# Windowed attention and a SiLU feed-forward on one core: idle matmuls placed by hand, a first d_ff group over both visits' tokens, and Strassen's scheme one tile earlier

## The chip, the cores and the metric

The kernel runs on one core of a Trainium2 chip. A core has a matrix engine (TensorE, PE in the profile; its weight loads are shown as PEld), a vector engine (VectorE, DVE), an engine for activation functions (ScalarE, ACT), a general engine (GpSimd, POOL), and a queue engine (SyncE, SP). They run side by side, each through its own list of instructions in order, and wait for each other on semaphores. Data move between the main memory and the core by DMA. Matmul results land in PSUM, which the kernel sees as eight banks of 512 fp32 columns in 128 partitions. The metric is the time of one execution on the device in microseconds (us), as the median of several runs.

## The reference

```python
# q, k, v: [8 batches, 8 heads, 576 positions, 64]
scores = scale * np.matmul(q, k.transpose(0, 1, 3, 2))
rel = pos[:, None] - pos[None, :]
mask = (rel >= 0) & (rel < 64)                  # 64 positions back, causal
attn = softmax(np.where(mask, scores, -1e9))
x = np.matmul(attn, v) -> [4608 tokens, 512]    # heads side by side
h = x @ w_in                                    # 512 -> 2048
g = h * (1.0 / (1.0 + np.exp(-h)))              # SiLU
out = g @ w_out                                 # 2048 -> 512, float32
```

## The kernel before

**Attention in visits.** The 4608 tokens are 72 blocks of 64, nine to a batch. A visit takes three blocks (visits 0 to 3) or four (the others) through a chain: scores on TensorE (line 317, in 32-row tiles of the array), exponential on ScalarE (L324), mask on VectorE (L333; the first three visits have the mask added in PSUM by four bias matmuls, L309, instead), attention times values on TensorE (L350, in 32-column tiles), then on VectorE a reciprocal (L356), the normalisation (L361, which empties the PSUM banks) and a transpose called the crossing (L369), which writes the tokens into the buffer `bridge`. Q and K are loaded by GpSimd's DMA queue (the first rows by SP and ScalarE) and turned on VectorE (L296, L299). Odd and even blocks need V rows in two layouts, so half of the rows are copied (L279).

**Feed-forward in tiles.** A tile is 512 tokens (eight blocks); there are nine, 0 to 8. The first layer (L379) takes 16 groups of 128 d_ff columns, each the sum of four matmuls over d_model; SiLU follows on ScalarE (L386), into slots of the buffer `g`. Tile 0 is cut up, since its tokens arrive visit by visit: groups 0 to 3 take the 192 tokens of visit 0, then those of visit 1 (`add_halves`, 32 matmuls of 192 columns), other groups take tokens 0 to 383 at once, and the last 192 tokens come later. The second layer has two forms. The plain one (L389) is 64 matmuls of 512 columns a tile, with copies of the result from PSUM (L394). The fast one, Strassen's scheme over 2 x 2 blocks (tokens in two halves, d_ff in two halves, d_model in two halves), is seven products in place of eight, 112 matmuls of 256 columns (L421). It needs sums of weights (L405, once, VectorE), sums of activations (L412, 16 a tile, VectorE), copies of partial results (L424, VectorE or ScalarE) and joins (L431, L433, VectorE). Tiles 0 to 2 use the plain form, tiles 3 to 8 (`FAST`) the fast one.

**What sets the order.** `Plan` (lines 16 to 137) is a list scheduler in the kernel's own Python. Operations are put into classes, each a queue in order; at each moment every engine takes, from the heads of the classes it serves, the one with the lowest number `first` (by default the class's `rank`) whose dependencies are done, whose gate is open and whose PSUM banks are free. Each operation has an assumed duration, from which the plan gets its clock. The order that comes out is what is issued. Attention stages run among the matmuls of the feed-forward; scores may run up to two tiles ahead (`gate_scores`). Until the last visit is done attention owns banks 0 to 3 and the feed-forward has 4 to 7. The plan also counts TensorE's instructions in `code` (an operation's own number, 2 for a matmul and its weight load) and lets TensorE stall where `code` passes 193, 449, 705 and so on, unless the instructions from there on, asked for 256 earlier, have come.

**Idle matmuls.** Until the first layer begins TensorE is given matmuls on a tile of zeros whose results nobody reads (`warm`, L719, 512 columns; `burn`, L724, four narrow ones). In the kernel before they are fillers: a class of the lowest priority, taken whenever TensorE would have nothing else by the plan's clock. There are 23 calls of `burn`, ten of `warm`, and up to 90 more of `warm` until the first d_ff matmul is planned. As issued, 92 narrow and 20 wide ones stand ahead of visit 0's scores, 9 between its scores and its values, 6 between visit 1's, and 4 between visit 1's values and visit 2's scores.

Of the kernel before, what the change touches and what calls it, by code (L numbers as in the profile page):

```python
# [15 lines left out]
class Plan:  # L16
# [13 lines left out]
    def add(self, cls, us, fn, deps=(), lat=0.1, gate=None, code=2, dma=None, pool=None, table=None, first=None, slow=0.0):  # L30
        op = dict(us=us, first=self.rank[cls] if first is None else first, fn=fn, deps=[d for d in deps if d is not None],
                  lat=lat, gate=gate, dma=dma, pool=pool, table=table, code=code, seen=None, n=self.count, until=[], bank=None, cls=cls, slow=slow)
        self.count += 1
        self.queues.setdefault(cls, []).append(op)
        return op

    def add_filler(self, n, cls, us, fn, parts, *args, **kw):
        for _ in range(n):
            op = self.add(cls, us, None, *args, **kw)
            op["until"], op["fn"], op["parts"] = [op], lambda e, op=op: fn(op), parts  # L40
        self.count -= n
# [10 lines left out]
    def run(self):  # L52
# [10 lines left out]
        while left:  # L63
# [6 lines left out]
            while moved:  # L70
                moved = False
                for e in engines:
# [28 lines left out]
                    if e == "PE":  # L101
                        m = {"s": "rows", "v": "cols"}.get(c[0] if c in ("s", "v", "s0", "v0") else "", "full")
                        if m != mode:
                            mode, us = m, us + 0.1
                        for x in range(193, code + op["code"], 256):
                            if x >= code:
                                t = us * (x - code) / op["code"]
                                us += max(0.0, chunk.get(x, 0.0) - now - t)
                                chunk[x + 256] = max(now + t, chunk.get(x, 0.0)) + (5.6 if now < 25 else 2.5)
# [22 lines left out]
                    left -= not c.startswith("warm")  # L132
# [8 lines left out]
def kernel(ctx, tc, q, k, v, w_in, w_out, out):  # L141
# [12 lines left out]
    NBR = 32  # L154
    NK, NV, NES, NOB = 2, 3, 3, 2
    RING = list(range(33, 40, 2)) + list(range(1, 32, 2))
    FAST = range(3, NTT)
# [42 lines left out]
                  s=1, v=0, moe=99, warm=200, warm2=201, exp=1, mask=1, inverse=0, norm=0.1, cross=0.2, turn=-1.25, cast=-4,  # L200
                  prime=-9, s0=-5.5, v0=-5.6, exp0=-4.6, inverse0=-4.3, norm0=-4.24, cross0=-4.22, turn0=-4.23, copy=1.5, copy0=-4.05),
# [251 lines left out]
    def add_turns(b, c=None):  # L453
        for Q in range(2):
            for kk in range(2):
                op = p.add("turn0" if b == 0 else "turn", {"DVE": 0.27 if b == 0 else 0.24 + 0.06 * (PARTS[b][c][1] - PARTS[b][c][0]) if b == 1 else 0.78}, lambda _, kk=kk, Q=Q: turn(b, kk, Q, c),
                           ([rows_in[(b, kk, c, Q)]] if b < 2 else rows_in[(b, kk, Q)]) + s_last.get(b - NK, []) + [c_k[b % NK]],
                           first=0.25 if (b, c) == (1, 2) else None if b > 1 else None, gate=p.late([rows_in[(b, kk, c, Q)]] if b < 2 else rows_in[(b, kk, Q)], 0.7) if b else None)
# [13 lines left out]
    def add_copies(b):  # L472
        for g in range(4):
            for up in (True, False):
                v_sh[(b, g, up)] = p.add("copy" if b else "copy0", {"DVE": 0.3} if (b, g, up) == (0, 2, True) else {"DVE": 0.3} if b == 0 and g == 3 else {"ACT": 0.66} if b > 1 or (b == 0 and g) else {"ACT": 0.66, "DVE": 0.3},
                                         lambda e, up=up, g=g: copy_v(e, b, g, up), v_in[(b, g)][0:1] + v_last.get(b - NV, []),
# [59 lines left out]
    def add_visit(vi):  # L536
# [7 lines left out]
        s = p.add("s" + z, {"PE": 0.05 * ns + (0.85 if first else 0.1)}, None,  # L544
# [3 lines left out]
        vi["s"] = s  # L548
# [5 lines left out]
        if not first:  # L554
            ma = p.add("mask", {"DVE": 0.16 + 0.00053 * 256 * ns}, lambda _: masking(vi), [ex, c_mask])
        pv = p.add("v" + z, {"PE": 0.05 * ns + 0.1}, None, [ma] + need_v(vi), pool=("two0", "two1", "two0")[i] if i < 3 else "at",
                   gate=(lambda: moe[20][0]["seen"] is not None) if i == 2 else None)
        pv["fn"] = lambda _: values(pv, vi)
        pv["code"] = 16 * ns
# [5 lines left out]
                   [no] + [x for n in range(vi["n0"], vi["n0"] + vi["nb"]) for x in br_free.get(n - NBR, [])])  # L565
# [38 lines left out]
    def add_halves(fts, gt):  # L604
        first = {}
        for i in range(2):
            for ft in fts:
                for c in range(NDC):
                    op = p.add("moe", {"PE": 0.0036 + 192 / 2400}, None, [o_done[3 * i], win[(ft, c)]], pool=None if c or i else "mp0")
                    bank = first.setdefault(ft, op)  # L610
                    op["fn"] = lambda _, bank=bank, ft=ft, c=c, i=i: first_layer(bank, 0, ft, c, 192 * i, 192 * i + 192, 192 * i)
                    moe.append((op, 1, 1 if c == 0 and i == 0 else -1, 0))
                if i:
                    slot, si = gt[ft]
                    op = p.add("silu", {"ACT": 0.18 + 384 * 0.00083}, lambda _, bank=bank, slot=slot: silu(bank, slot, 0, 384), [op], table="silu")
                    si.append(op)
                    bank["until"] = [op]
# [99 lines left out]

    def warm(op):
        nc.tensor.matmul(ps[:, op["bank"][0], 0:128 * op["parts"]], lhsT=idle, rhs=idle.unsqueeze(1).to_broadcast([128, op["parts"], 128]),  # L719
                         start=True, stop=True)  # L720

    def burn(op):
        for j in range(4):
# [144 lines left out]
```

## Time and profile before

| | |
|---|---|
| median of 3 runs | 293.4 us (293.4 to 294.83) |
| the profiled execution | 291.75 us |
| its span, first to last instruction | 290.0 us |
| TensorE busy (share of the span) | 280.6 us (97%), 4019 matmuls |
| VectorE busy | 165.3 us (57%) |
| ScalarE busy | 167.9 us (58%) |
| GpSimd busy | 117.6 us (41%) |
| mean granted TensorE clock | 0.994 |

Times in the profile are us from the span's start unless marked ns. A row of a timeline or of a group names the engine, the operation, the tile written, an arrow, the tiles read, the shapes and a count; square brackets hold the idle time before it and what ended that. The chain is followed back from the last instruction: at each step to what released it, else to the instruction before it on its engine; its rows give start, length and what. "Issue" is time in which the engine waited for nothing that the profile shows. A row of stretches gives from:to and the length, then the engines' busy times. Some matmul records are missing from a trace, so counts can be a few short, and the length of a single matmul includes its way through the pipeline.

### The profile page before, as it was taken

The page shows a single profiled execution, that of the slowest core. Times are in us where ns is not written, and L with a number is a line of the kernel's source. Part 1 is how long each engine was busy: PE and PEld are TensorE (multiplying, and loading weights), DVE is VectorE, ACT ScalarE, POOL GpSimd, SP SyncE. Part 2 cuts the span into 40 slices and gives each one's busy share as a digit, 9 for nine tenths or more (in the row PEclk, how much of TensorE's full clock was granted, in tenths as well). Part 3 has the DMA queues.
Part 4 walks back from the last instruction along what each step waited for, and adds up shares of the span by engine and source line. Part 5 has one row for each costly group of instructions (what it writes and reads, how often), then busy time and mean ns, then how long its engine had stood idle before and what let it go on. Part 6 is the DMA issues. An engine that isn't in the chain of part 4 may idle for free.

```text
span 290.0 us, 9229 instructions
## 1 busy us (share of the span) xinstructions
PE 280.6 (97%) x4019; PEld 178.0 (61%) x4031; DVE 165.3 (57%) x306; ACT 167.9 (58%) x261; POOL 117.6 (41%) x181
## 2 busy tenths in 40 slices
PE   8789999999999999999999999999999999999995
PEld 4247764796544445447854785478547854784584
DVE  3583416992955258646874687459446944332433
ACT  2629871899747763768256844683468346416610
POOL 8965848989987988697500000000000000000000
PEclk9799999999999999999999999999999999999999
DMA  9999999999999999999961003000300030003013
GB/s 149 127 187 190 190 183 141 201 164 127 173 222 157 174 161 181 222 128 186 97 184 48 2 2 147 0 5 2 145 2 3 3 148 0 2 3 141 2 36 109
DMA packets 88840, 31.51 MB, mean 109 GB/s; under 512 B 75872, under 2 KB 84064, under 8 KB 88800
## 3 DMA queue, kind: packets, MB, share of 16 engines
q0 software_dynamic: 81600, 18.00, 67.3%
q1 hardware_dynamic: 6016, 11.75, 12.4%
q10 hardware_dynamic: 1184, 1.18, 1.4%
q8 instruction: 31, 0.51, 0.7%
q14 instruction: 9, 0.07, 0.1%
HBM read 36.70 MB, written 9.44 MB: 159 GB/s over the span
## 4 chain that ended last, share of the span: by engine, by line
PE 91%; DMA 3%; DVE 2%; ACT 1%; issue 1%; ACTq 0%; DVEq 0%
PE ps L379 42%; PE ps L421 26%; PE ps L389 12%; PE ps L350 4%; PE ps L317 4%; PE ps L719 2%; DMA gsum<-in_k_dram 2%; DMA natq<-in_q_dram 1%; DVE ob L361 1%; ACT e L324 1%; ACTq L263 0%; DVE qt L299 0%; ACT L386 0%; DVE kt L299 0%; DVE bridge L369 0%
## 5 line engine op out<-in xcount | busy, mean ns | idle before, releaser
L379 PE MATMUL ps<-bridge,w_in_sb 128*128 128x512 bf16 (+3 forms) x720 | 127.0, 337 | 0.4 <-ACT g L386 0.4
L386 ACT ACTIVATE g<-ps 128x512 bf16<-128x512 f32 (+3 forms) x176 | 89.7, 520 | 42.4 <-PE ps L379 41.2
L379 PEld LDWEIGHTS <-w_in_sb 128*128 128x128 bf16 x720 | 67.5, 98 | 55.9 <-issue 0.7
L412 DVE TENSOR_TENSOR gsum<-g 128x512 bf16<-128x512 bf16 x48 | 20.2, 422 | 48.3 <-ACT g L386 48.3
L324 ACT ACTIVATE e<-ps 128x2048 bf16<-128x2048 f32 (+1 forms) x19 | 34.0, 1787 | 19.4 <-PE ps L317 19.1
L389 PE MATMUL ps<-w_out_sb,g 128*128 128x512 bf16 x180 | 41.5, 379 | 1.5 <-issue 1.3
L421 PEld LDWEIGHTS <-gsum 128*128 128x128 bf16 x384 | 37.1, 98 | 4.5
L421 PE MATMUL ps<-g,gsum 128*128 128x256 bf16 x288 | 36.4, 273 | 0.0
L333 DVE TENSOR_TENSOR e<-e,mask 128x2048 bf16<-128x2048 bf16 (+1 forms) x16 | 19.2, 1200 | 25.6 <-ACT e L324 25.5
L246 POOL DMA_DIRECT2D natk<-in_k_dram x48 | 29.1, 627 | 8.3 <-DMA natk<-in_k_dram 5.1
L257 POOL DMA_DIRECT2D vo<-in_v_dram x32 | 28.6, 907 | 5.3 <-DMA w_out_sb<-in_moe_w_out_dram 2.2
L389 PEld LDWEIGHTS <-g 128*128 128x128 bf16 x192 | 17.8, 98 | 20.4
L246 POOL DMA_DIRECT2D natq<-in_q_dram x48 | 29.2, 635 | 2.5 <-issue 0.6
L421 PEld LDWEIGHTS <-g 128*128 128x128 bf16 x288 | 27.4, 98 | 4.0
L424 ACT COPY part<-ps 128x256 f32<-128x256 f32 x23 | 8.6, 373 | 29.4 <-PE ps L421 26.3
L421 PE MATMUL ps<-w_out_sb,g 128*128 128x256 bf16 x192 | 23.0, 273 | 0.0
L361 DVE TENSOR_TENSOR ob<-ps,rc 128x1024 bf16<-128x1024 f32 (+1 forms) x19 | 22.1, 1161 | 0.4
L369 DVE STREAM_TRANSPOSE bridge<-ob 128x1024 bf16<-128x1024 bf16 (+1 forms) x19 | 22.1, 1171 | 0.3
L433 DVE TENSOR_TENSOR ot<-ps,part 128x256 f32<-128x256 f32 (+1 forms) x30 | 13.7, 469 | 8.1 <-ACT part L424 4.4
L317 PEld LDWEIGHTS <-kt 32*128 32x128 bf16 x1152 | 10.5, 92 | 9.5 <-issue 6.9
L317 PE MATMUL ps<-qt,kt 32*128 32x64 bf16 x1152 | 12.8, 190 | 2.8 <-DVE kt L299 1.8
L350 PEld LDWEIGHTS <-e 128*32 128x32 bf16 x1152 | 11.2, 98 | 6.2 <-issue 3.2
(60 smaller groups left out, 218.0 us busy)
## 6 DMA issues: line engine op xcount, KB each, us to landing
out_dram<-ot SPq DMA_DIRECT2D x32, 256.0 KB, 2.6
vo<-in_v_dram POOLq DMA_DIRECT2D x32, 128.0 KB, 5.0
natq<-in_q_dram POOLq DMA_DIRECT2D x48, 72.0 KB, 4.6
natk<-in_k_dram POOLq DMA_DIRECT2D x48, 72.0 KB, 4.5
ve<-vo SPq DMA_DIRECT2D x10, 264.0 KB, 5.1
w_in_sb<-in_moe_w_in_dram POOLq DMA_DIRECT2D x8, 256.0 KB, 8.4
w_out_sb<-in_moe_w_out_dram POOLq DMA_DIRECT2D x8, 256.0 KB, 7.1
out_dram<-ot ACTq DMA_DIRECT2D x6, 128.0 KB, 1.9
```

The lines of the kernel that those rows point to most:

```text
L246: nc.gpsimd.dma_start(out=nats[kk][b % NK][r, h // 4].rearrange("p c x -> p (c x)").rearrange("p (t x) -> p t x", x=2 * D), in_=(q, k)[kk] ...
L257: nc.gpsimd.dma_start(out=vos[b % NV][:, g, :, 0:D], in_=v[b, :, 128 * g:128 * g + 128].rearrange("h p d -> p h d"))
L317: nc.tensor.matmul(sc[:, j, 64 * s:64 * s + 64], lhsT=kts[b % NK][r, Q, 64 * t:64 * t + 128, h], rhs=qts[b % NK][r, Q, 64 * t:64 * t + 64, h],
L324: nc.scalar.activation(out=es[vi["i"] % NES][:, :, 0:ns].rearrange("p j s i -> p j (s i)"), in_=ps[:, op["bank"][0]:op["bank"][0] + 4, 0:6 ...
L350: nc.tensor.matmul(pv[32 * j:32 * j + 32, sub // k, sub % k], lhsT=e[:, j, s, 32 * u:32 * u + 32], rhs=w[:, 4 * Q + j].rearrange("p (x i) ...
L361: nc.vector.tensor_mul(obs[vi["i"] % NOB][:, 0:4 * vi["nb"]].rearrange("p s (i x) -> p (s i) x", i=2).rearrange("p (b k) x -> p b k x", b= ...
L369: nc.vector.transpose(out=br.rearrange("p n Q u h i -> p (n Q u h) i"), in_=ob.rearrange("p s (h d) -> p (s h) d", h=2))
L379: nc.tensor.matmul(ps[:, bank["bank"][0], at:at + hi - lo], lhsT=w_in_sb[:, c, ft * 128:(ft + 1) * 128], rhs=bridge[:, n0 + lo // 64:n0 + ...
L386: nc.scalar.activation(out=g[:, lo:hi], in_=ps[:, bank["bank"][0], 0:hi - lo], func=ACTF.Silu)
L389: nc.tensor.matmul(ps[:, bank["bank"][0]], lhsT=gall[:, slot, m * 128:(m + 1) * 128], rhs=w_out_sb[:, f], start=(f == 0), stop=(f == NFT - 1))
L412: (nc.vector.tensor_sub if i else nc.vector.tensor_add)(out=t[i], in0=a, in1=b)
L421: nc.tensor.matmul(ps[:, bank["bank"][0], lo:lo + 256], lhsT=lhs, rhs=rhs, start=first, stop=last, skip_group_check=True)
```

## The change

- The fillers go. `add_idle` puts a fixed number of idle matmuls into a new class `lead`, which also holds, in this order, the scores and values of visits 0 and 1 and the scores of visit 2. A class is taken in order, so the order of all these on TensorE is now written down: 42 idles of 128 columns, 4 + 9 of 512 columns, scores 0, 7 idles, values 0, scores 1, 9 idles, values 1, 4 idles, scores 2, 4 idles. Visit 2's values keep a class of their own, open once 21 matmuls of the first layer are planned.
- The first d_ff group (`add_quads` in place of `add_halves`) takes the 384 tokens of visits 0 and 1 in one matmul: 16 matmuls of 384 columns, ordered so that all four groups do the first half of d_model before the second. It depends on both visits' crossings and on visit 2's scores.
- `FAST` begins at tile 2.
- Smaller: visit 0's crossing must follow a copy of V rows (batch 0, group 2), whose copies get a higher priority; visit 0's crossing goes ahead of its normalisation's rank; the turns of batches 4 and 5 get rank 0.3 in place of -1.25, behind the reciprocal, normalisation and crossing of later visits; the assumed time of an instruction refill is 5.0, 6.0 or 2.5 us in place of 5.6 or 2.5; the assumed time of the first scores falls.

```diff
-    FAST = range(3, NTT)
+    FAST = range(2, NTT)
...
-                  s=1, v=0, moe=99, warm=200, warm2=201, exp=1, mask=1, inverse=0, norm=0.1, cross=0.2, turn=-1.25, cast=-4,
-                  prime=-9, s0=-5.5, v0=-5.6, exp0=-4.6, inverse0=-4.3, norm0=-4.24, cross0=-4.22, turn0=-4.23, copy=1.5, copy0=-4.05),
+                  s=1, v=0, moe=99, exp=1, mask=1, inverse=0, norm=0.1, cross=0.2, turn=-1.25, cast=-4,
+                  prime=-9, lead=-5.6, v0=-5.5, exp0=-4.6, inverse0=-4.3, norm0=-4.24,cross0=-4.25,turn0=-4.23, copy=1.5, copy0=-4.05),
...
-                           first=0.25 if (b, c) == (1, 2) else None if b > 1 else None, gate=...
+                           first=0.25 if (b, c) == (1, 2) else 0.3 if b in (4, 5) else None, gate=...
...
-    def add_visit(vi):
+    def add_visit(vi, idle=0):
...
-        s = p.add("s" + z, {"PE": 0.05 * ns + (0.85 if first else 0.1)}, None,
+        s = p.add("lead" if first else "s", {"PE": 0.05 * ns + (0.3 if first else 0.1)}, None,
...
-        pv = p.add("v" + z, {"PE": 0.05 * ns + 0.1}, None, [ma] + need_v(vi), ...
+        add_idle(idle, 4, 0.217)
+        pv = p.add("lead" if i < 2 else "v" + z, {"PE": 0.05 * ns + 0.1}, None, [ma] + need_v(vi), ...
...
+    def add_quads(fts, gt, hi):
+        bank = {}
+        for Q in range(2):
+            for ft in fts:
+                for c in (2 * Q, 2 * Q + 1):
+                    op = p.add("moe", {"PE": 0.0036 + hi / 2400}, None, [o_done[0], o_done[3], visits[2]["s"], win[(ft, c)]], pool=None if c else "mp0" if fts[0] == 0 else "mp")
+                    b = bank.setdefault(ft, op)
+                    op["fn"] = lambda _, b=b, ft=ft, c=c: first_layer(b, 0, ft, c, 0, hi)
...
+    def add_idle(n, parts, us):
+        for _ in range(n):
+            op = p.add("lead", {"PE": us}, None, [c_idle], pool="any", lat=0.0)
+            op["until"], op["parts"], op["fn"] = [op], parts, lambda _, op=op: warm(op)
...
-    p.add_filler(23, "warm", {"PE": 0.07}, burn, 0, [c_idle], pool="any", lat=0.0, code=8)
-    p.add_filler(10, "warm", {"PE": 0.43}, warm, 4, [c_idle], pool="any", lat=0.0)
-    p.add_filler(90, "warm2", {"PE": 0.217}, warm, 4, [c_idle], pool="any", lat=0.0,
-                 gate=lambda: moe[0][0]["seen"] is None)
-    add_visit(visits[0])
-    add_visit(visits[1])
+    add_idle(42, 1, 0.109)
+    add_idle(4, 4, 0.43)
+    add_idle(9, 4, 0.217)
+    add_visit(visits[0], 7)
+    add_idle(0, 4, 0.217)
+    add_visit(visits[1], 9)
+    add_idle(4, 4, 0.217)
     add_visit(visits[2])
+    add_idle(4, 4, 0.217)
```

47 lines of the change are left out of this document (16 added, 31 removed).

## The prediction

> **What bounds the kernel now.** I read the page first: the span, the clock that TensorE was granted in 40 slices, and what the chain of waits consists of.
>
> ```profile
> span 290.0 us, 9229 instructions
> ...
> PEclk9799999999999999999999999999999999999999
> ...
> PE 91%; DMA 3%; DVE 2%; ACT 1%; issue 1%; ACTq 0%; DVEq 0%
> ```
>
> TensorE is 91% of the chain. Time can be won in two ways only: fewer TensorE microseconds in the steady part, or an earlier start of the d_ff matmuls, which run without a break from then on. The second digit of the clock row is the only low one. So the next view is the chain in order of time, for the lead-in (start, length, what):
>
> ```profile
> 10.26 0.48 PE ps L317 x39
> 10.74 3.73 PE ps L719 x9
> 14.47 0.59 PE ps L350 x41
> ...
> 15.49 0.97 DVE ob L361
> ...
> 16.50 1.46 PE ps L719 x6
> 17.96 0.54 PE ps L350 x39
> ...
> 20.35 1.02 issue
> 21.36 0.42 PE ps L317 x30
> 21.79 2.33 PE ps L379 x27
> 24.12 0.55 PE ps L350 x39
> 24.66 13.60 PE ps L379 x117
> ...
> 260.45 13.81 PE ps L379 x64
> ```
>
> L317 is scores, L350 attention times values, L719 idle matmuls, L379 the first layer. Three things hold the first layer back to 21.7: nine idle matmuls of 3.73 us ahead of visit 0's values; visit 1's chain; and 1.02 us in the middle of visit 2's scores in which TensorE waited for nothing that is recorded. The exponentials and some vector work (timeline) and the clock (stretches; after the length come the busy times of TensorE, its weight loads, VectorE, ScalarE and GpSimd with counts, the granted clock, the DMA share and GB/s):
>
> ```profile
> 11.38 1.44 ACT L324 ACTIVATE e<-ps 128x1536 bf16<-128x1536 f32 x1
> 16.33 1.45 ACT L324 ACTIVATE e<-ps 128x1536 bf16<-128x1536 f32 x1 [3.51 <-PE ps L317]
> 18.92 0.46 DVE L299 STREAM_TRANSPOSE kt<-natk 128x192 uint32<-128x192 uint32 x1
> 20.20 0.98 DVE L369 STREAM_TRANSPOSE bridge<-ob 128x768 bf16<-128x768 bf16 x1
> 2.50:3.00 0.50, 0.50 (x2) 0.15 (x1) 0.50 (x4) 0.37 (x1) 0.50 (x1) 1.00 1.05 311
> 4.00:4.50 0.50, 0.50 (x4) 0.26 (x3) 0.00 (x0) 0.13 (x1) 0.50 (x1) 1.00 1.10 254
> 7.35:10.77 3.42, 1.66 (x55) 0.89 (x53) 2.79 (x8) 2.75 (x5) 2.87 (x5) 1.00 1.30 119
> 10.77:14.18 3.41, 3.41 (x9) 1.07 (x8) 1.17 (x3) 2.04 (x3) 3.41 (x6) 0.50 1.48 138
> ```
>
> The pace of the idle matmuls doubles near 4.0 (two, then four in half a microsecond). After 3.42 us in which TensorE was busy for 1.66, the next 3.41 ran at clock 0.50. Visit 0's exponential was over at 11.38 + 1.44 = 12.82, but its values started at 14.47, behind the nine.
>
> **The change, part by part.** This execution took 291.75 us (span 290.0 and 1.75 around it); the runs' median, 293.4, is 1.65 above it. I apply differences in the span to the median.
>
> **1. Strassen's scheme for tile 2.** I compare the stretch of tile 2's second layer with tile 3's, which has the scheme already, by the stretches view, with rows for the product's price and vector work:
>
> ```profile
> 99.71:117.16 17.45, 16.77 (x381) 8.89 (x386) 10.57 (x13) 9.27 (x8) 14.89 (x23) 1.00 1.58 186
> 131.86:147.03 15.17, 15.17 (x370) 13.13 (x370) 12.57 (x22) 6.75 (x7) 9.00 (x13) 1.00 1.30 124
> 131.92 0.62 PE ps L317 x57
> 248.22 12.23 PE ps L421 x112
> L421 PEld LDWEIGHTS <-gsum x384: 95/98/99, 135.0 to 286.1; 128*128 128x128 bf16 x192
> L412 DVE TENSOR_TENSOR gsum<-g x48: 417/422/426, 122.2 to 275.8; 128x512 bf16<-128x512 bf16 x48
> L405 DVE TENSOR_TENSOR g<-w_out_sb x4: 647/650/651, 58.8 to 64.6; 128x1024 bf16<-128x1024 bf16 x4
> 103.69 1.23 DVE L333 TENSOR_TENSOR e<-e,mask 128x2048 bf16<-128x2048 bf16 x1 [7.38 <-ACT e L324]
> L433 DVE TENSOR_TENSOR ot<-ps,part x30: 385/424/692, 138.0 to 286.5; 128x256 f32<-128x256 f32 x24, 128x512 f32<-128x512 f32 x6
> 110.42 1.20 DVE L369 STREAM_TRANSPOSE bridge<-ob 128x1024 bf16<-128x1024 bf16 x1
> ```
>
> Tile 2 has 64 products of 512 columns, three scores stages and two value stages in 17.45 us, 0.68 of it TensorE idle. Tile 3 has 112 products of 256 columns, two scores stages and two value stages in 15.17. With a third scores stage (0.62) tile 2 would take 15.79: **1.66 us less**. The two prices agree: 64 x 13.81/64 = 13.81 against 12.23 is 1.58, and the rest is idle time where TensorE changes the kind of tiling.
>
> VectorE pays: 16 token sums (16 x 0.42 = 6.8 at most), six joins (4 x 0.42 + 2 x 0.69 = 3.1) and its share of six copies of partial results, some 11 us in all. It has 7.38 us idle just before 103.69, after the first layer's activations, and 17.45 - 10.57 = 6.9 in the stretch; the four copies of the output that go were on ScalarE. The weight sums end by 66 in the kernel before, so they aren't late at 99.7. The turns of batches 4 and 5 (four each) fall behind the normalisation; behind them wait only GpSimd's loads for batches 6 and 7, two batches ahead. SP's queue gets the same four stores of the tile, some of them later; nothing but later stores stands behind them. I take 0 on the path, because tile 3 bears the same work without a TensorE gap; the VectorE rival is the upper bound.
>
> The 112 products carry 48 more weight loads. A load is 98 ns beside 12.23/112 = 109 ns a product, and 13.13 us of loads lie inside tile 3's 15.17: hidden, 0. The Trainium skill's "TensorE: Matmul & The Clock Gate" (The mechanism) says that weight loads overlap matmuls in flight only where the row groups differ, which full 128-row loads never do. By that rule the change would make the kernel slower, 296.0 (the last rival); tile 3's stretch speaks against it.
>
> **2. The lead-in.** In the kernel's order on TensorE: 42 idles of 128 columns, 13 of 512, scores 0, 7 idles, values 0, scores 1, 9 idles, values 1, 4 idles, scores 2, 4 idles, first layer. A wide idle is 13.81/64 = 0.216 us, and twice that at clock 0.50.
> Fill: 0.108 each (a quarter of 0.432) from 1.0 to about 4.0, so 27 or 28; the other 15 at 0.054 (0.098 if the loads bind), then 13 x 0.216: over at 7.6 to 8.2, against 7.6 before. Scores 0 wait for the turns until 10.26 either way, and end at 10.74: 0.
> Clock: as little busy time falls between 7.35 and 10.77 as before, so I let the clock drop again. Seven idles at 0.43 are 3.0: over at 13.75, past the exponential's 12.82. Values 0, half of them at half speed, end at 14.5, not 15.06: 0.5 earlier. Scores 1 took 1.27 (15.06 until exponential 1 at 16.33), so they end at 15.75.
> The nine idles wait for banks 2 and 3, which values 0 used, so for the normalisation: 14.5 + 1.4 (15.06 to 16.46 before) = 15.9. Nine end at 17.85, where six ended at 17.96, although exponential 1 is over at 15.8 + 1.45 = 17.3: three more idles eat 0.45 of the 0.5. Values 1 end at 18.4, four idles at 19.25; the turns that scores 2 need are over by then (18.92 + 0.46 in the kernel before, and visit 0's crossing, ahead of them, is 0.5 earlier). The copy of value rows that must now precede visit 0's crossing already did: 0.
> The 1.02 us: I count matmuls up to it, 92 + 20 + 52 + 9 + 48 + 52 + 6 + 48 + 4 + 4 + 16 = 351, with a weight load each 702 instructions; the planner's code puts a refill border at 705. Instructions do come by DMA (queue row, 18.7 to 19.9):
>
> ```profile
> q8 instruction: 1, 0.02, 4.9%
> ```
>
> That packet answers the border before, 449, passed seven instructions into scores 1, at about 15.0; the resume at 21.36 makes a refill 6.4 us. With 92 narrow matmuls gone and fewer idles, TensorE has 331 matmuls, 662 instructions, behind it when the first layer starts: scores 2 run through in 1.27, and end at 20.5, not 21.78. Border 449 is now values 1's start (446 before it), its refill asked for at 10.4 and there at 16.8, a microsecond ahead. Border 705 comes 21 matmuls into the first layer, at about 24.8; refill 17.9 + 6.4 = 24.3. Just covered.
> First layer: it now needs visit 1's crossing too, once 20.20 + 0.98 = 21.18, now about 20.95; the four idles end at 21.4. Start **21.4 instead of 21.7: 0.3 us**. Exponential 2 moves 1.2 earlier, so the activation table is there before the first banks are full.
> Sixteen of 384 columns replace 32 of 192: 32 x 2.33/27 = 2.76 against 16 x 0.159 = 2.54 (117 matmuls in 13.60, 69 of them narrow at 0.086): **0.2 us**.
> Sum: 1.66 + 0.3 + 0.2 = 2.2. Profiled run 289.6; median 293.4 - 2.2 = **291.2**.
> Bounds of the lead-in: the clock stays up where it dropped before: values 0 at 12.9, first layer near 20.4, 1.3 won. The refill at 705 takes 2 us longer: about 1.5 lost.
>
> **The rivals.**
> *The lead-in gives nothing (292.0 to 291.7).* If the clock doesn't drop in either kernel, nine idles take 1.9, both start values 0 at 12.9; then six idles end at 16.3 and nine at 16.9, and both first layers start at 20.3 to 20.4. Only Strassen is left: 293.4 - 1.66 = 291.7. For it: the runs differ by more than a microsecond among themselves. Against: the profiled drop. The Trainium skill's same page (What's actually happening) says that the clock's activity window runs freely and isn't set by the kernel's start, which would make this differ from run to run; no run here shows it yet.
> *The refill stall only moves (292.3).* Border 705 is met with 0.5 us to spare; a refill of 8 us stalls 1.1. For it: the 6.4 is one measurement, at another moment. Against: nothing but that number.
> *VectorE too late in tile 2 (slower, 294 to 299).* Sums, joins and copies go ahead of masks and crossings. Tile 3's first layer, at about 115, needs visit 8's crossing, over at 110.42 + 1.20 = 111.6 now, 111.1 with the lead-in's gain: slack 3.9. A delay d of that crossing costs d - 3.9, so the kernel turns slower from d = 3.9 + 2.2 = 6.1; with all 11 us ahead of it, 11 - 6.1 = 4.9 slower. Less the 7.38 idle, 3 to 4 us stand ahead of it, just the slack. Against it also: tile 3 carries 12.57 of such work in 15.17 with TensorE never idle.
> *Weight loads not hidden (slower, 296.0).* If each product paid its load, 112 x (98 + 109) ns = 23.2 us stood against 64 x (98 + 216) = 20.1: 293.4 + 3.1 - 0.5. This is what the page's rule quoted above would do.
>
> **How the numbers follow.** Half a per cent, 1.5 us, is about what a measurement can tell. Forecast 0.48, all faster; lead-in gives nothing 0.22, of which 0.13 faster and 0.09 same; refill stall 0.10, same; VectorE 0.11, of which 0.09 slower and 0.02 same; loads 0.01, slower; something unseen 0.08 (0.05 more gain with the clock up, 0.01 same, 0.02 slower). Faster 0.66, same 0.22, slower 0.12. The range reaches from the clock staying up (1.66 + 1.3 + 0.2 = 3.2: 290.2, and a little more) to the refill and VectorE cases: 289.8 to 293.8; the likeliest alone 290.4 to 292.
>
> **What would show it.** Right: 112 more products on L421; tile 2's second layer near 15.8 with no idle; scores 2 in one piece; values 0 by 13.8; first L379 at 21.4 or sooner. Wrong: a wait of TensorE on VectorE between 99 and 120, a stall after the 705th instruction, the first layer later than 21.7, or a second low digit in the clock row.

## The result and the profile after

The changed kernel takes **290.71 us** (median of 17 runs, 289.43 to 291.79); the kernel before, run beside it, 293.4 (17 runs, 291.24 to 296.41). The ratio is **0.9912, with a 95% interval of 0.9886 to 0.9938**: faster by about 2.6 us. (Ratios leave out runs more than 1.5% above the fastest of their kernel; here that is one of before, 296.41.) The forecast was 291.2, within 289.8 to 293.8.

The two profiled executions stand closer together than the medians: 291.16 us now (span 289.4) against 291.75 (span 290.0). The sum of the prediction, made against that one execution, said 289.6. So the median was met and the profiled sum was not. The page of the changed kernel, with the lines that answer to those shown of before (span, granted clock in 40 slices, the chain by engine):

```profile
span 289.4 us, 9221 instructions
PEclk9999999999999999999999999999999999999999
PE 87%; DMA 5%; ACT 3%; POOL 3%; issue 1%; DVE 0%; POOLq 0%; ACTq 0%
```

The low digit of the clock row is gone. TensorE is less of the chain than it was (91%), and transfers are more (3% before): something now waits for loads. The lead-in shows where, in the timeline of TensorE (start, length, operation; square brackets hold the idle time before a row and what ended it):

```profile
5.45 3.65 PE L719 MATMUL ps<-idle 128*128 128x512 bf16 x13
...
9.67 0.55 PE L311 MATMUL ps<-qt,kt 32*128 32x64 bf16 x48
10.15 1.69 PE L719 MATMUL ps<-idle 128*128 128x512 bf16 x7
11.80 0.32 PE L344 MATMUL ps<-ve,e 128*32 128x66 bf16 x16
...
13.91 2.13 PE L719 MATMUL ps<-idle 128*128 128x512 bf16 x9 [0.26 <-DVE ob L355]
15.97 0.32 PE L344 MATMUL ps<-vo,e 128*32 128x66 bf16 x16
...
18.13 0.55 PE L311 MATMUL ps<-qt,kt 32*128 32x64 bf16 x48
18.61 1.04 PE L719 MATMUL ps<-idle 128*128 128x512 bf16 x4
19.49 2.76 PE L373 MATMUL ps<-bridge,w_in_sb 128*128 128x384 bf16 x16
22.70 0.50 PE L373 MATMUL ps<-bridge,w_in_sb 128*128 128x384 bf16 x2 [0.45 <-DMA w_in_sb<-in_moe_w_in_dram]
23.96 0.66 PE L373 MATMUL ps<-bridge,w_in_sb 128*128 128x384 bf16 x3 [0.76 <-DMA w_in_sb<-in_moe_w_in_dram]
...
37.48 0.55 PE L311 MATMUL ps<-qt,kt 32*128 32x64 bf16 x48
```

(In this kernel L311 is scores, L344 values, L373 the first layer, L383 the plain second layer, L415 Strassen's products, L363 the crossing.) The first layer starts 2.2 us earlier than before (21.72), but stops twice for w_in's columns. Visit 3's scores, the first steady landmark, come at 37.48 against 38.20: 0.7 us are left.

Tile 2 and tile 3 in stretches (from:to, length, then busy us of TensorE, weight loads, VectorE, ScalarE, GpSimd with counts; clock; DMA share; GB/s). Each stretch is a second layer or a first layer; the four lie between the scores that open tile 2's second layer and those that open tile 4's. First after, then before, of which two rows stand in the prediction:

```profile
99.00:114.17 15.17, 15.17 (x369) 13.14 (x369) 13.09 (x23) 6.75 (x7) 13.83 (x22) 1.00 1.53 149
114.17:128.08 13.91, 13.91 (x67) 6.18 (x65) 7.71 (x18) 9.92 (x16) 10.28 (x16) 1.00 1.43 208
128.08:145.65 17.57, 16.17 (x433) 13.79 (x433) 13.15 (x21) 9.02 (x9) 13.07 (x20) 1.00 1.49 142
145.65:160.42 14.77, 14.77 (x138) 6.79 (x139) 11.03 (x20) 9.86 (x16) 0.69 (x1) 1.00 0.54 121
```

```profile
117.16:131.86 14.70, 14.70 (x131) 6.68 (x130) 8.28 (x16) 10.81 (x17) 12.04 (x19) 1.00 1.54 164
...
147.03:161.00 13.97, 13.97 (x74) 6.22 (x75) 7.51 (x17) 9.92 (x16) 0.00 (x0) 1.00 0.36 115
sum 61.29, PE 60.60 PEld 34.92 DVE 38.94 ACT 36.75 POOL 35.93; mean PE 15.15 PEld 8.73 DVE 9.73 ACT 9.19 POOL 8.98
```

Tile 2's second layer takes 15.17 us and never idles. Tile 3's grew from 15.17 to 17.57: a third scores stage moved into it (433 matmul records instead of 370), TensorE is busy 16.17 - 15.17 = 1.00 us longer, and it idles 1.40 us. Together the four stretches of after are 61.42 us against 61.29. In this execution Strassen's gain is gone by tile 4. What ate it, in tile 3's timeline:

```profile
132.36 0.68 PE L311 MATMUL ps<-qt,kt 32*128 32x64 bf16 x64 [0.22 <-ACT e L318]
...
139.59 0.23 PE L344 MATMUL ps<-ve,e 128*32 128x66 bf16 x5 [1.19 <-issue]
```

1.19 us in the middle of a values stage, in which TensorE waited for nothing that is recorded, as in visit 2's scores before. From 160.42 on both kernels need 129.0 us.

Two theories went to the experiments. **The fill's**: the gain comes from the fill, which keeps the clock up and lets the first rows of Q and K land earlier; Strassen's 1.66 us are mostly given back in tile 3. **Strassen's**, as the prediction had it: the gain is that of tile 2, and the lead-in is worth a few tenths.

### The profile page after: what moved, and what is told of

The parts are those of the page before. It is cut to its first block, busy times and chain, and to the rows that moved or that the text cites. A ratio compares the mean times of both kernels' runs of the same rounds, so it can differ in the third digit from the quotient of the medians.

```text
span 289.4 us, 9221 instructions
## 1 busy us (share of the span) xinstructions
PE 280.7 (97%) x4004; PEld 184.2 (64%) x4011; DVE 175.8 (61%) x331; ACT 167.1 (58%) x260; POOL 117.9 (41%) x181
## 4 chain that ended last, share of the span: by engine, by line
PE 87%; DMA 5%; ACT 3%; POOL 3%; issue 1%; DVE 0%; POOLq 0%; ACTq 0%
PE ps L373 41%; PE ps L415 29%; PE ps L383 9%; PE ps L344 4%; PE ps L311 3%; DMA w_in_sb<-in_moe_w_in_dram 3%; DMA natq<-in_q_dram 2%; ACT e L318 1%; POOL vo L251 1%; POOL w_in_sb L276 1%; ACT L318 0%; ACT L380 0%; ACT g L380 0%; POOL ve L254 0%; POOL natk L245 0%
## 5 line engine op out<-in xcount | busy, mean ns | idle before, releaser
L373 PE MATMUL ps<-bridge,w_in_sb 128*128 128x512 bf16 (+3 forms) x704 | 127.3, 340 | 1.6 <-DMA w_in_sb<-in_moe_w_in_dram 1.2
L373 PEld LDWEIGHTS <-w_in_sb 128*128 128x128 bf16 x704 | 66.4, 98 | 58.5 <-DMA w_in_sb<-in_moe_w_in_dram 2.0
L406 DVE TENSOR_TENSOR gsum<-g 128x512 bf16<-128x512 bf16 x56 | 23.4, 418 | 49.1 <-ACT g L380 49.0
L415 PEld LDWEIGHTS <-gsum 128*128 128x128 bf16 x448 | 43.2, 98 | 5.2
L415 PE MATMUL ps<-g,gsum 128*128 128x256 bf16 x336 | 42.6, 273 | 0.0
L415 PEld LDWEIGHTS <-g 128*128 128x128 bf16 x336 | 31.8, 98 | 4.6
L418 ACT COPY part<-ps 128x256 f32<-128x256 f32 x26 | 9.7, 373 | 36.1 <-PE ps L415 36.1
L383 PE MATMUL ps<-w_out_sb,g 128*128 128x512 bf16 x121 | 27.6, 379 | 0.9 <-issue 0.8
L415 PE MATMUL ps<-w_out_sb,g 128*128 128x256 bf16 x224 | 26.8, 273 | 0.0
L363 DVE STREAM_TRANSPOSE bridge<-ob 128x1024 bf16<-128x1024 bf16 (+1 forms) x19 | 22.2, 1173 | 0.2
L427 DVE TENSOR_TENSOR ot<-ps,part 128x256 f32<-128x256 f32 (+1 forms) x35 | 16.1, 470 | 9.2 <-PE ps L415 4.6
L383 PEld LDWEIGHTS <-g 128*128 128x128 bf16 x128 | 11.9, 98 | 13.8
L415 PE MATMUL ps<-g 128*128 128x256 bf16 x112 | 15.9, 273 | 0.0
L344 PEld LDWEIGHTS <-e 128*32 128x32 bf16 x1152 | 11.3, 98 | 7.0 <-issue 4.2
L719 PE MATMUL ps<-idle 128*128 128x128 bf16 (+1 forms) x79 | 14.0, 355 | 1.3 <-DVE idle L231 1.0
```

The source lines that it names most:

```text
L344: nc.tensor.matmul(pv[32 * j:32 * j + 32, sub // k, sub % k], lhsT=e[:, j, s, 32 * u:32 * u + 32], rhs=w[:, 4 * Q + j].rearrange("p (x i) ...
L363: nc.vector.transpose(out=br.rearrange("p n Q u h i -> p (n Q u h) i"), in_=ob.rearrange("p s (h d) -> p (s h) d", h=2))
L373: nc.tensor.matmul(ps[:, bank["bank"][0], at:at + hi - lo], lhsT=w_in_sb[:, c, ft * 128:(ft + 1) * 128], rhs=bridge[:, n0 + lo // 64:n0 + ...
L383: nc.tensor.matmul(ps[:, bank["bank"][0]], lhsT=gall[:, slot, m * 128:(m + 1) * 128], rhs=w_out_sb[:, f], start=(f == 0), stop=(f == NFT - 1))
L406: (nc.vector.tensor_sub if i else nc.vector.tensor_add)(out=t[i], in0=a, in1=b)
L415: nc.tensor.matmul(ps[:, bank["bank"][0], lo:lo + 256], lhsT=lhs, rhs=rhs, start=first, stop=last, skip_group_check=True)
```

## The experiments

All ratios are to the kernel before, run on the same chip.

| kernel | median us (runs) | ratio, 95% interval |
|---|---|---|
| e1 before again | 292.8 (12) | 1.003, 0.9994 to 1.0065 |
| e2 Strassen alone | 291.8 (12) | 0.9975, 0.9943 to 1.0007 |
| e3 lead-in alone | 290.35 (12) | 0.9951, 0.9923 to 0.9979 |
| e4 fill alone | 290.14 (12) | 0.9942, 0.992 to 0.9965 |
| e5 more narrow idles first | 291.6 (11) | 0.9969, 0.9938 to 1.0 |
| e6 narrow idles last | 291.44 (11) | 0.9959, 0.9925 to 0.9994 |
| e7 the change again | 289.33 (5) | 0.9897, 0.9846 to 0.9948 |
| e8 w_in earlier | 289.32 (5) | 0.9887, 0.9845 to 0.9929 |
| e9 lead-in alone again | 290.01 (12) | 0.9949, 0.9926 to 0.9972 |
| e10 the change, third time | 290.48 (12) | 0.9944, 0.9914 to 0.9973 |
| e11 w_in earlier, no Strassen in tile 2 | 290.0 (12) | 0.9941, 0.9913 to 0.9968 |
| e12 fewer idles | 290.3 (12) | 0.9944, 0.9917 to 0.9971 |

e1 to e4 shared a chip, e5 to e8 another, e9 to e12 a third.

### e1: the kernel before, once more

No edit; a second copy of the kernel before, to see how far executions of one kernel differ.

> The kernel before, unchanged, to see how its own executions differ. Theory A (the prediction): they differ little in the lead-in; the clock drop of 3.4 us at half speed behind the first scores is in nearly every execution (mean granted clock 0.994), and the ratio to itself is 1.000 within 0.004. Theory B (the two profiles side by side): the drop is there in some executions only and costs about 1.5 us where it is, so mean clocks of 0.994 and 1.000 both occur and the spans of the first are longer by 1 to 2 us.

292.8 us, the same as before within 0.7%. Its profiled execution took 294.41 with the clock at 1.0 throughout, and stalls that the first profile of the same code does not have:

```profile
19.28 0.42 PE L317 MATMUL ps<-qt,kt 32*128 32x64 bf16 x32 [0.80 <-issue]
...
78.06 0.32 PE L350 MATMUL ps<-ve,e 128*32 128x66 bf16 x16 [0.62 <-DVE ob L361]
...
92.16 0.32 PE L350 MATMUL ps<-ve,e 128*32 128x66 bf16 x16 [1.29 <-DMA ve<-vo]
```

So stalls of a microsecond come and go between executions with the landing of loads. A single profile can't carry a difference below that; medians and stretches must.

### e2, e3, e4: the change in parts

e2 is the kernel before with one line of the change:

```diff
-    FAST = range(3, NTT)
+    FAST = range(2, NTT)
```

> The kernel before with Strassen's scheme from tile 2 on and nothing else. Theory A: 1.66 us faster, ratio 0.9943, tile 2's second layer 15.8 us with three scores stages or 15.2 with two. Theory B: the products are saved in tile 2 but a refill of instructions in tile 3 gives it back (in the changed kernel's profile the stretch from tile 2's scores to tile 4's takes 61.42 us against 61.29 before), so no gain: ratio 0.998 to 1.000.

e3 is the changed kernel without that line (`FAST = range(3, NTT)`).

> The changed kernel with Strassen's scheme from tile 3 on, as before, so only the lead-in, the first d_ff group and the ranks are changed. Theory A: 0.5 us faster, ratio 0.998. Theory B: the lead-in carries nearly all of the 2.7 us, ratio 0.991 to 0.993, and the clock stays at 1.000 in every execution.

e4 is the kernel before with the fill of the change alone; all else, fillers and first group included, as before:

```diff
-    p.add_filler(23, "warm", {"PE": 0.07}, burn, 0, [c_idle], pool="any", lat=0.0, code=8)
-    p.add_filler(10, "warm", {"PE": 0.43}, warm, 4, [c_idle], pool="any", lat=0.0)
+    p.add_filler(42, "warm", {"PE": 0.109}, warm, 1, [c_idle], pool="any", lat=0.0)
+    p.add_filler(4, "warm", {"PE": 0.43}, warm, 4, [c_idle], pool="any", lat=0.0)
```

> The kernel before with only its first fillers exchanged: 42 idle matmuls of 128 columns and 4 of 512 at the planned cold price in place of 92 narrow and 10 wide ones; what follows is filled by the plan as before. Instructions ahead of the first layer fall from 768 to 650, so the stall of 1.02 us within the third scores should go. Theory A: that stall was half of the lead-in's 0.5 us: ratio 0.998. Theory B: the fill decides whether the clock drops, and how long; mean clock 1.000 in every execution and ratio 0.993 to 0.996.

Strassen alone gave 0.25%, not to be told from nothing. The lead-in alone gave 0.5%, and the two lines of the fill gave as much as the whole lead-in (0.58%, visit 3's scores at 36.44; e3 36.54; before 38.20). Idles placed by hand, group matmuls over both visits' tokens and the new priorities add nothing that can be measured. That speaks for the fill's theory, though not all its numbers came: e2's ratio is nearer to its 0.998 to 1.000 than to the other theory's 0.9943 (the interval reaches both), and e3's 0.9951 lies between the two forecasts. That the fill carries the gain is shown by e4; by which of its effects is not.

e2's profile shows one more thing, in the timeline of TensorE and, second, of VectorE:

```profile
117.16 2.76 PE L379 MATMUL ps<-bridge,w_in_sb 128*128 128x512 bf16 x12 [1.08 <-DVE bridge L369]
```

```profile
108.49 1.22 DVE L361 TENSOR_TENSOR ob<-ps,rc 128x1024 bf16<-128x1024 f32 x1
109.63 0.77 DVE L296 STREAM_TRANSPOSE qt<-natq 128x576 uint32<-128x576 uint32 x1
111.61 0.69 DVE L431 TENSOR_TENSOR ot<-part,ps 128x512 f32<-128x512 f32 x1 [1.21 <-ACT part L424]
...
115.87 2.36 DVE L369 STREAM_TRANSPOSE bridge<-ob 128x1024 bf16<-128x1024 bf16 x2
```

Visit 8's tokens were normalised at 109.7, but their crossing came at 115.87, behind turns of Q and K, joins and visit 9's normalisation; tile 3's first layer waited 1.08 us for it. This is the prediction's rival "VectorE too late in tile 2", in its place. In the whole change the crossing comes behind the normalisation and one turn:

```profile
108.05 1.21 DVE L355 TENSOR_TENSOR ob<-ps,rc 128x1024 bf16<-128x1024 f32 x1
109.18 0.77 DVE L290 STREAM_TRANSPOSE kt<-natk 128x576 uint32<-128x576 uint32 x1
109.87 1.20 DVE L363 STREAM_TRANSPOSE bridge<-ob 128x1024 bf16<-128x1024 bf16 x1
```

Of the edits, the rank 0.3 for the turns of batches 4 and 5 is the likely reason: it lets crossings overtake turns. That edit alone was not run, so its part is argued from the order, not shown.

### e5, e6: where the narrow idles stand

Both keep the kernel before and its late fillers. e5 has 40 calls of `burn` at the start instead of 23 (68 more matmuls); e6 begins with 33 matmuls of 128 columns, then has 16 calls of `burn` (64 narrow ones), then 4 wide ones.

```diff
-    p.add_filler(23, "warm", {"PE": 0.07}, burn, 0, ...)
+    p.add_filler(40, "warm", {"PE": 0.07}, burn, 0, ...)
```

> The kernel before with 40 calls of the narrow idle matmuls instead of 23 (the plan then places 5 wide ones less ahead of the first scores): the fill is as long, but all later work comes 122 instructions later in TensorE's list. Laid over the times of the kernel before, its refill borders (every 256 instructions) leave seven pairs less than 6.5 us apart between 50 and 145 us, 8.8 us short in sum; moved so, they leave four, 3.7 us short. Theory C (a refill takes up to 6.5 us while loads run, so the place of the borders decides what stalls): ratio 0.995 to 0.998, though the first rows still land as late as before. Theory D (what counts is that the first rows land earlier and the clock stays up; the borders don't matter): ratio 1.000.

```diff
-    p.add_filler(23, "warm", {"PE": 0.07}, burn, 0, ...)
-    p.add_filler(10, "warm", {"PE": 0.43}, warm, 4, ...)
+    p.add_filler(33, "warm", {"PE": 0.109}, warm, 1, ...)
+    p.add_filler(16, "warm", {"PE": 0.07}, burn, 0, ...)
+    p.add_filler(4, "warm", {"PE": 0.43}, warm, 4, ...)
```

> The fill of 128-column matmuls first (33) and then 16 calls of the narrow ones, so that later work stands within 10 instructions of its place in the kernel before, but the first refill isn't asked for until about 5 us, when the first rows of Q and K have landed. Theory C: the steady stalls are back, 0.998 to 1.000, with the first turn at 7.7 us as in the run with the new fill alone. Theory D: 0.994 like that run.

Neither changed the time by half a per cent. e5's ratio lies where theory C put it, e6's between the two theories, and both intervals are too wide to decide. But the traces tell two things apart. First, when the first rows land. The queue that brings instructions (`q8`: packets, MB, share) moves its first packet in the kernel before between 4 and 6 us, in the changed kernel between 9 and 15, as the DMA views of these stretches say; the first cast of Q follows the rows' landing. The queue's row before and after:

```profile
q8 instruction: 1, 0.02, 4.0%
```

```profile
q8 instruction: 1, 0.02, 1.0%
```

And the first cast in VectorE's timeline, before, after, in e5 and in e6:

```profile
7.98 0.49 DVE L268 CAST natq<-gsum 128x384 bf16<-128x384 f32 x1 [4.35 <-DMA gsum<-in_q_dram]
```

```profile
6.68 0.36 DVE L262 CAST natq<-gsum 128x384 bf16<-128x384 f32 x1 [3.04 <-DMA gsum<-in_q_dram]
```

```profile
7.89 0.36 DVE L268 CAST natq<-gsum 128x384 bf16<-128x384 f32 x1 [4.26 <-DMA gsum<-in_q_dram]
```

```profile
6.65 0.36 DVE L268 CAST natq<-gsum 128x384 bf16<-128x384 f32 x1 [3.02 <-DMA gsum<-in_q_dram]
```

With 92 narrow idles first, TensorE comes to its 193rd instruction near 4 us (in the changed kernel near 10, among scores 0), so the next block is fetched while the first rows of Q and K are on their way. In the four profiles in which the narrow ones come first (before, e1, e2, e5) that packet moves before 6 us and the first cast starts at 7.58 to 7.98; in the ten with later or wider ones it moves after 6, and the cast starts at 6.63 to 6.88 (e12: 7.12). e6 holds nearly the same number of instructions as before, only later: early rows. So it is the moment, not the number. That the packet itself delays the rows fits all fourteen and was not tried apart from the idles.

Second, the clock. Of 35 runs of e1, e2 and e5, 13 have a mean clock of 0.993 or 0.994, as the profiled kernel before had (0.994), and of the 84 runs of the kernel before that the ratios of e1 to e12 use, 21 have 0.992 to 0.994. Of 99 runs with the fill of the change (after, e3, e4, e7 to e12) none is below 0.997. e6, with early rows but 64 narrow idles near the end of its fill, has two of 11. In stretches, the one that had 1.66 us busy of 3.42 before, and the one behind it, in the changed kernel:

```profile
7.35:10.77 3.42, 3.42 (x64) 1.73 (x62) 2.51 (x7) 2.60 (x5) 2.89 (x5) 1.00 1.14 119
10.77:14.18 3.41, 3.15 (x107) 1.77 (x106) 3.03 (x6) 2.07 (x3) 3.28 (x6) 1.00 1.52 147
```

The Trainium skill's "TensorE: Matmul & The Clock Gate" (What's actually happening) says that the activity window runs freely. The share of 21 in 84 agrees: one and the same order of idles loses the clock in some runs and not in others.

Yet the clock is a small part of the gain. Chip by chip, those 21 runs are 1.0, 0.9 and 0.3 us longer on average than the other runs of the kernel before; in a quarter of the runs that makes, by estimate, 0.2 us on average. On e4's chip these runs of the kernel before take 291.96 us on average and the 25 without the drop 291.77; e4's take 290.26. So 1.5 of the 1.7 us remain where the clock stayed up.

Nor is the lead-in itself shorter where the clock stayed up: visit 3's scores come at 37.03, 36.06 and 37.88 in e1, e2 and e5, and at 36.44 to 37.48 with the fill of the change and the old order of loads (after, e3, e4, e7, e9, e10). What differs is what follows. From those scores to the end e1 needs 255.6 us and e2 254.4, with waits of 0.62 and 1.29, and of 0.76 and 0.70, near 78 and 92 us; before, e5, e6 and the nine profiles with the fill of the change need 250.9 to 252.5 and have no wait above 0.6 us there. The runs fit this: on that chip the shortest of before's 35 took 289.89 us and the shortest of e4's 12 took 289.8, the longest 294.78 and 291.74. So the fill seems to make long executions rarer rather than the best one shorter. How often the old fill brings these waits, and whether the late rows cause them, was not measured and stays open.

### e7, e8: the change again, and w_in's columns earlier

e7 is the changed kernel. e8 moves one load in GpSimd's queue ahead of two loads of V:

```diff
+    add_w_in(1)
     add_v(0, 3)
     add_v(0, 4)
-    add_w_in(1)
```

> The changed kernel, unchanged, beside the others on this chip: ratio 0.991 within 0.003. Theory C expects a stall of TensorE at a refill in tile 2's or tile 3's second layer in this execution too (256 instructions take 3.5 to 4.6 us there), and waits for the weights of the first layer before 25 us.

> The changed kernel with the second pair of w_in loads moved ahead of the last two loads of V of batch 0. If the landing of those weights bounds the lead-in (1.2 us of waits in the changed kernel's profile), the waits before 25 us go and the kernel is 0.5 to 1.2 us faster than the changed one. If visit 2's values, which need that V, become the next late thing, or the loads just change places, no gain.

Equal in time: 289.33 and 289.32. In e8's timeline of TensorE the wait for w_in is gone, and visit 3's scores come at 35.73 (e7: 37.36):

```profile
19.07 4.55 PE L373 MATMUL ps<-bridge,w_in_sb 128*128 128x384 bf16 x27
...
24.09 11.71 PE L373 MATMUL ps<-bridge,w_in_sb 128*128 128x384 bf16 x101
35.73 0.55 PE L311 MATMUL ps<-qt,kt 32*128 32x64 bf16 x48
...
141.42 0.26 PE L311 MATMUL ps<-qt,kt 32*128 32x64 bf16 x9 [1.19 <-issue]
```

So the landing of w_in does bound the lead-in after the change, but taking that bound away did not show in the medians, although e8's span was 1.3 us below e7's. The stall in tile 3 is there in both (e7: 0.93 us at 142.65). In the list of TensorE's instructions, these two stalls stand at number 4545, that of the changed kernel's profile at 4289, and the one of before at 705; all are 193 plus a multiple of 256, where the plan puts its borders. e1, with the plain form in tile 2, has such a stall in tile 3 too (0.75 us at 143.04), so it does not take Strassen's scheme in tile 2.

### e9 to e12: side by side on one chip

e9 is e3 again, e10 the changed kernel. e11 is e8 with `FAST = range(3, NTT)`. e12 is e8 with fewer idles:

```diff
-    add_visit(visits[1], 9)
+    add_visit(visits[1], 5)
     add_idle(4, 4, 0.217)
     add_visit(visits[2])
-    add_idle(4, 4, 0.217)
+    add_idle(1, 4, 0.217)
```

> The changed kernel with Strassen's scheme from tile 3 on, as before the change, beside the whole change on one chip. Tile 2's second layer takes some 17.4 us again (the whole change: 15.17), with three scores stages in it. Theory A (a refill of instructions in tile 3 gives back most of Strassen's gain): this kernel is at most 0.7 us slower than the whole change. Theory B (the gain of 1.66 us is kept in most executions, and the stalls seen were chance): it is 1.2 to 1.8 us slower.

> The changed kernel, to be read against the other three of this chip. Theory A: a stall of 0.8 to 1.3 us that ends in 'issue' between 135 and 145, 256 instructions being passed there in less than 5.5 us; from scores 3 to the end 251.6 to 252.0. Theory B: no such stall, and 250.3 to 250.8.

> w_in's second block loaded ahead of V's, with Strassen's scheme from tile 3 on. The first layer has no wait for w_in, scores 3 near 35.7 to 36.0 against 36.5 for the same kernel without the edit. If what the lead-in gains is kept to the end: 0.5 to 0.8 us faster than the lead-in alone. If the loads of batches 1 to 4, all of them later by then, only bring a later wait (a steady stall for V's or Q's rows between 40 and 150): equal to it.

> w_in's second block first, 5 idles ahead of visit 1's values in place of 9, and 1 in place of 4 ahead of the first layer; Strassen's scheme from tile 2 on. The prediction said that the idles ahead of values 1 outlast exponential 1: then values 1 start at 14.8 in place of 15.5 (exponential 1 ends at 14.75), scores 2 when their last turn is over, near 16.9, and the first layer at 18.3 to 18.6 in place of 19.07, behind visit 1's crossing; the clock stays at 1.0. About 0.5 us faster than the whole change and 0.5 less at scores 3 than with the weights first. If the turns or the crossing hold the first layer anyway, or the clock drops: no gain.

All four lie between 290.0 and 290.48. **e10 against e9** is Strassen in tile 2 and nothing else: 290.48 against 290.01, no gain (each interval is some 0.25% to 0.3% wide to either side). Yet e10's profiled execution is the one in which Strassen's gain survives. Its stretch from tile 2's scores to tile 4's, in two rows, and e9's:

```profile
98.27:127.34 29.07, 29.07 (x433) 19.31 (x434) 20.78 (x39) 16.67 (x23) 23.69 (x36) 1.00 1.46 176
127.34:158.52 31.18, 30.85 (x562) 20.51 (x562) 24.05 (x41) 18.87 (x24) 13.96 (x22) 1.00 1.11 138
sum 60.25, PE 59.92 PEld 39.81 DVE 44.83 ACT 35.54 POOL 37.64; mean PE 29.96 PEld 19.91 DVE 22.42 ACT 17.77 POOL 18.82
```

```profile
98.83:160.06 61.23, 61.23 (x945) 34.94 (x946) 38.93 (x65) 36.75 (x48) 38.29 (x58) 1.00 1.28 156
```

TensorE's work falls by 61.23 - 59.92 = 1.31 us, and it idles 60.25 - 59.92 = 0.33 in e10: 0.98 us kept. In the changed kernel's own profile 1.40 idle, in e2 61.35 - 59.89 = 1.46: nothing kept. What differs is when the instructions come. The border at 4033 was passed at 132.77 in the changed kernel and at 132.03 in e10. The packet that it asks for moved in the changed kernel between 136.5 and 138.0, in e10 between 134.3 and 135.5, which the DMA views of these stretches show beside the packets of GpSimd's loads (`q0`):

```profile
q0 software_dynamic: 1006, 0.24, 173.8%
q8 instruction: 1, 0.02, 5.1%
```

```profile
q0 software_dynamic: 278, 0.07, 58.7%
q8 instruction: 1, 0.02, 5.0%
```

TensorE needs 5.64 us for the 256 instructions that it has left (132.77 to 138.41). In the changed kernel the next ones were there after 6.82 us (139.59), in e10 it passed the border at 137.49 without a stop. So the stall is instructions that come late: their packet moved some 1.5 us later behind its border (136.5 - 132.77 against 134.3 - 132.03), with more packets of loads beside it. That it waited for these fits the rows and was not tried. From the first of these scores to the last the changed kernel's profile needs 61.35 us and e7's 61.05; without their stalls of 1.19 and 0.93 that is 60.16 and 60.12, about e10's 60.25. Of the changed kernel's three profiles two have the stall that theory A of these expectations names (1.19 and 0.93 us); the third has none, and needs 287.6 - 36.73 = 250.9 us from scores 3 to the end, close to theory B's 250.3 to 250.8. So neither holds for every execution: in these three profiles the gain is kept where the instructions come in time.

**e11 against e9**: scores 3 at 35.88 against 37.29, span 287.7 against 289.1, medians 290.0 and 290.01. As with e8, a gain in the profile and none in the medians. What takes it back in other executions was not seen and stays open.

**e12**: fewer idles gave nothing. Two rows of its timeline say why:

```profile
16.21 0.28 PE L344 MATMUL ps<-vo,e 128*32 128x66 bf16 x12 [0.72 <-issue]
...
19.97 0.48 PE L311 MATMUL ps<-qt,kt 32*128 32x64 bf16 x40 [1.40 <-DVE kt L293]
```

Visit 1's values began at 15.28, 0.7 earlier than in the changed kernel, and stopped after four matmuls at border 449 until 16.21. With nine idles there this stop is gone, or short (0.31 us in e11). Then scores 2 waited 1.40 us for the last turn, which stood on VectorE behind visit 1's normalisation and crossing. No version was found that beats the change.

## Why the prediction was right and where it was wrong

**The number.** 291.2 against 290.71, in the range, and faster, as the largest chance said. That the total came so close is luck, for its parts were wrong in opposite directions: the lead-in, sized at 0.3 + 0.2 us, is worth 0.5% or 1.5 us (e3, e9), and Strassen, sized at 1.66, between nothing and about a microsecond. Weighted by one over the square of their intervals, the three measurements of the whole change give 0.9922 and the two of the lead-in 0.9950; the difference, 0.8 us, is uncertain by about as much, and the one direct comparison has the other sign.

**Strassen for tile 2.** Tile 2 itself went as worked out: 15.17 us without a gap, the third scores stage apart. The failed step is the comparison of tile 2 alone, with "I take 0 on the path" for the rest: the third scores stage was not late work in tile 2 but moved to tile 3, and the saving over both tiles is 1.31 us of TensorE, not 1.66. The stage was priced at 0.62; with it in tile 3, TensorE was busy 1.00 us longer than before. Tile 3 then asks for 256 instructions in 5.64 us while loads still run. **The refill stall only moves** was a rival at 0.10, and this is its mechanism, but it went to tile 3 and not to border 705, which was covered as predicted (no stop near 24.5).

**Weight loads.** Hidden: 13.14 us of loads in a stretch of 15.17 without idle time. The rule weighed against the trace in the prediction, by which they would be paid, does not hold here.

**VectorE.** No wait in the whole change, with 13.09 us busy in tile 2's 15.17. The rival was nearer than its slack of 3.9 us said: with Strassen alone it cost 1.08 us (e2). The prediction priced the new rank of the turns at nothing, since only loads wait behind them; the order of VectorE makes it the likely guard of this tile.

**The lead-in.** "As little busy time falls between 7.35 and 10.77 as before, so I let the clock drop again" is the step that failed. The fill ended later than the 7.6 to 8.2 worked out (at 9.1; the idles ran at half speed until 6.8, not 4.0), the rows landed 1.3 us earlier, and TensorE was busy for all of that stretch. In e7 the fill ended at 7.58, and TensorE was still busy for 3.02 of the 3.42 us, so a late end of the fill was not needed for it. "Scores 0 wait for the turns until 10.26 either way" failed with it: they ran at 9.67. Values 0 started at 11.80, earlier than the bound with the clock up (12.9). The rival "lead-in gives nothing" rested on a clock that drops in neither kernel; it drops in some runs of the one and in none of the other, which explains some 0.2 us of the gain. What explains the rest is open: the traces point to waits near 78 and 92 us that only executions with the old fill showed.

**What was late next.** Behind the first layer's start, at 19.49 instead of 21.4, the prediction named visit 1's crossing and the four idles. Next in line were w_in's columns (0.45 and 0.76 us in the profile) and, behind the nine idles, the refill that e12 met. The 1.02 us in scores 2 went, as predicted. The **0.2 us** for the wider first group is not visible: the 16 wide matmuls stand 0.1625 us apart (2.60 in all), the narrow ones 0.0825 (2.64 for 32), and e4 without the wide ones is as fast as e3.

## What to carry to other kernels

Count instructions like bytes: where matmuls are small, see how many of them stand between two refills, and which loads share the queues at that moment; a faster scheme with more instructions can hand its gain to waits for instructions (1.19 us in tile 3 of the profile). Price a change over the whole stretch up to the next common landmark, since a scheduler moves the work that no longer fits. Warm-up matmuls have a second effect beside the clock: narrow ones use up instructions early, and where they stood first the refill fell among the first loads, which landed later. And a drop of the clock that one profile shows need not be what the median pays for: sort the runs by their clock first.

## What the runs showed that was not expected

- Instructions came late only up to 143 us, and GpSimd's loads end soon after (0.69 us of its work lies behind 145.65). In tile 3 a refill took 6.82 us from the border before to the resume (139.59 - 132.77) in one execution and at most 5.46 (137.49 - 132.03) in another of the same kernel. The Trainium skill's "Runtime: NRT & Kernel Launch" (Instruction fetch mechanics) calls the cost of crossing such a border mostly hidden; here up to 1.19 us stood there in dense small matmuls, and how much changes from run to run: 1.02 us at border 705 before, 0.23 at the same place in e2.
- The clock dropped behind a stretch in which TensorE was busy for 1.66 of 3.42 us, so not only after an idle one. In e1 the stretch of that length in the same place behind the rise of its clock (7.20 to 10.61; it rose at 3.79, before at 3.95) holds 1.83 us, and the clock stayed up.
- Executions of one program differ by several stalls of 0.6 to 1.3 us: e1's profile, at full clock, has three behind 70 us (0.62 for VectorE's normalisation, 1.29 for V's rows, 0.75 in which nothing recorded was waited for) that the first profile of the same code lacks. A lead-in that is 1.4 to 1.6 us shorter in the profile (e8, e11) did not move the medians.
